# A new order for every engine, the activation table loaded first, layer-norm statistics in groups, two gates read from PSUM, and a last tile in three parts

## The chip, the cores and the metric

The kernel runs on one core of a Trainium2 chip. The core has a matrix engine (TensorE, PE in the profile; its weight loads are listed as PEld), a vector engine (VectorE, DVE), a scalar engine (ScalarE, ACT), a general engine (GpSimd, POOL), and a queue engine (SyncE, SP) that issues most DMAs. Each engine takes its own instructions in program order and waits on semaphores for the others. The metric is the device time of one execution in microseconds (us), the median of three runs.

## What is computed

```python
def _A_ref(q, k, v, shift_k, ssm_k, ssm_D):      # S = 2048 rows, D = 640 channels
    k_shift = sum(k_pad[:, t:t + S, :] * shift_k[:, ks - 1 - t] for t in range(4))
    kv = k_shift * v
    y = irfft(rfft(kv, 2 * S) * rfft(ssm_k, 2 * S))[:S]   # long convolution, per channel
    y = y + kv * ssm_D
    return q * y

x = A_q
h = x + _A_ref(layernorm(x), A_k, A_v, A_shift_k, A_ssm_k, A_ssm_D)
h2 = h + mish(layernorm(h) @ w1 + b1) @ w2               # 640 -> 1728 -> 640
```

`_A_ref` gets the normalised x as q, so the convolution's result y is multiplied ("gated") by the normalised row and added to x. Then comes an ordinary feed-forward block with the activation Mish.

## The kernel before

The long convolution is done as a two-step Fourier transform written as matrix products. The 640 channels are five blocks of 128, put in three chunks: chunk 0 is block 0, chunk 1 is blocks 1 and 2, chunk 2 is blocks 3 and 4. The 2048 rows are 16 tiles of 128. The program is a list of named operations; each name stands for a group of instructions on one engine. In the order in which data passes:

- `k1pe`, `k1ev`, `dadd` (L540, L374/L372, L549): transpose the filter, evict it from PSUM, add the direct term. `s1kpe`, `s1kev` (L466/467): first transform step of the filter; `s2kpe`, `s2kev` (L573): its second step, 22 groups of 6 frequencies. `sw` (L588/589): DMAs that make a copy of the filter's spectrum with even and odd partitions exchanged.
- `ktpe`, `ktev`, `ktsh` (L496, L505): transposed k. `wsh` (L423): the shift weights. `kspe` (L519/520): the four-tap shift as matmuls; `kv` (L525): its result times v, ten operations on DVE.
- `s1vpe`/`s1vev` and `s2vpe`/`s2vev` (L466/467, L609, evicted at L372 or L374): both transform steps of kv, 20 groups each.
- `p2` and `p1` (L629, L625): the complex product of spectrum and filter, 40 operations on bf16 data in SBUF. `p1_c_i` needs `p2_c_i`, because it overwrites what `p2_c_i` reads. They run on DVE, four of them on POOL.
- `i1pe`/`i1ev` (L660/661): first inverse step, 20 groups; those of a chunk need all its `p1` and `p2`. `gate` (L636) is a small POOL operation that waits for all products.
- per tile t: `ln1_t` (L697 to L699: two statistics, an aggregation, and the addition of epsilon on DVE), `ln1pt` (L703, L704: power -1/2 and a scaled mean on POOL), `lnxt` (the normalised tile, ACT or POOL); `i2pa/b/c` (L724: second inverse step), `yt` (eviction, L372/L374), `wbt` (times `lnx`, L735), `ht` (plus x, L739), `bnt` (L744 to L746), `powt` (POOL, L749), `hct` (L754), `trpet` (L762), `trevt` (eviction).
- the feed-forward block in units of 256, 256, 512, 512, 512 rows: `m1pe` (L797, L793), `hb` (Mish on ACT, L806), `m2pe` (L818), `res` (DVE adds the matmul's result in PSUM to x, L824), `d_out` (the DMA out). The last tile, 15, is in two halves of 320 columns: `m2a`, `resa`, `d_outa`, then `m2b`, `resb`, `d_outb`.

PSUM is used as a ring of four tiles of 1024 fp32 columns. An operation that needs one waits until an earlier holder is evicted; tiles of `i2p` may hold three at most.

The order of the work is written out by hand at the head of the file as one long list, `ORDER`, of `name:engine` (t is PE, a is ACT, v is DVE, p is POOL, d is the SP queue's DMAs). A planner walks the list, gives each operation a start time from a table of costs, assigns the PSUM tiles, and the operations are then emitted sorted by these start times. So within an engine the list decides the order; between engines the start times decide which instruction is emitted first, and dependencies (who waits for whom on a tile) are found from the emitted order:

```python
order = _schedule(ops)
order.sort(key=lambda o: (o.start, seq[id(o)]))
```

ScalarE evaluates functions from a table. The program builder puts a table load before the first copy and another before the first Mish; `warm` is a Mish of two columns that is there only to place the second load.

Of the kernel before, what the change touches and what calls it, by code (L numbers as in the profile page):

```python
# [36 lines left out]
ktsh2:p s2kev_15:a kspe4_1:t kv4_1:v s2kpe_14:t s2kev_14:a sw1_0:d kspe2_0:t s2kpe_13:t s2kev_13:a s2kpe_16:t kspe1_0:t kv2_0:v s1vpe2_0:t s2kev_16:a
s1vev2_0:a kv1_0:v s1vpe2_2:t s1vev2_2:v s1vpe2_3:t s1vev2_3:a s1vpe1_0:t s1vev1_0:v s1vpe1_3:t s1vev1_3:a s1vpe1_2:t s1vev1_2:a s1vpe1_1:t s1vpe2_1:t
s1vev2_1:a s2kpe_20:t s1vev1_1:v s2kpe_17:t s2kev_17:a s2kev_20:v kspe3_0:t s2kpe_18:t s2vpe1_2:t kspe0_1:t s2kev_18:a s2vev1_2:a sw1_1:d p2_1_2:p
s2vpe1_1:t s2vev1_1:a kv3_0:v s2vpe1_3:t s2vev1_3:a kspe4_0:t ln1_1:v s2vpe1_4:t s2vev1_4:a kv0_1:v kv4_0:v p2_1_3:v s2vpe1_6:t s2vev1_6:a kspe0_0:t  # L40
s2vpe1_0:t s2vev1_0:a p1_1_2:v p1_1_3:p kv0_0:v kspe3_1:t d_x2:d warm:a kv3_1:v sw0_1:d s2vpe1_7:t s2vev1_7:a s1vpe4_1:t s1vev4_1:a p2_1_1:v p2_1_0:v
# [8 lines left out]
i1pe2_7:t ln1_6:v d_small:p i1ev1_6:a gate:p lnx3:a i1ev2_5:a ln1p2:p ln1p1:p ln1_7:v i1ev2_7:a i1pe2_1:t i1ev2_1:a i1pe2_4:t i1ev2_4:v ln1_4:v  # L50
i1pe2_2:t i1ev2_2:a i1pe2_0:t i1ev2_0:a lnx1:p i1pe2_3:t i1ev2_3:v lnx2:p ln1p7:p ln1p6:p lnx6:p i1pe2_6:t ln1_12:v i2pa0:t i2pb0:t i2pa1:t ln1p4:p
i2pb1:t i1ev2_6:a lnx0:p i2pc1:t y1:a i2pc0:t y0:v lnx4:p b1pe:t wb1:v i2pa12:t i2pb12:t c_b1:a i2pc12:t y12:a wb0:v h0:v bn0:v i2pa3:t i2pb3:t
i2pc3:t y3:a i2pa2:t i2pb2:t i2pc2:t h1:p bn1:v i2pa6:t pow0:p hc0:v i2pb6:t y2:a i2pc6:t y6:a i2pa8:t i2pb8:t i2pc8:t y8:a i2pa11:t i2pb11:t i2pc11:t
y11:a i2pa5:t i2pb5:t i2pc5:t y5:a i2pa4:t i2pb4:t i2pc4:t y4:a i2pa13:t i2pb13:t i2pc13:t y13:a i2pa15:t i2pb15:t i2pc15:t y15:a pow1:p trpe0:t hc1:v
wb2:v i2pa7:t trev0:a i2pb7:t trpe1:t i2pc7:t trev1:v y7:a wb3:v i2pa10:t i2pb10:t i2pc10:t y10:a m1pe0_0:t m1pe0_2:t hb0_0:a m1pe0_4:t hb0_4:a
hb0_2:a h2:v bn2:v h3:p bn3:v pow2:p hc2:v m1pe0_1:t hb0_1:a pow3:p hc3:v m1pe0_6:t wb4:v h4:p trpe2:t trpe3:t lnx7:a trev2:v m1pe0_3:t hb0_6:a
ln1_10:v bn4:v ln1_5:v m1pe0_5:t wb7:p h7:p trev3:a m1pe1_1:t m1pe1_3:t wb6:v hb0_3:a h6:v hb1_1:a hb0_5:a ln1p5:p bn6:v m1pe1_4:t lnx5:a pow4:p bn7:v
hb1_3:a wb5:v h5:v bn5:v hb1_4:a m1pe1_6:t hb1_6:a pow7:p pow6:p hc4:v hc6:v hc7:v m2pe0:t trpe4:t trev4:a trpe6:t ln1_8:v trev6:a ln1p8:p ln1p10:p
ln1_11:v m1pe1_0:t ln1p11:p trpe7:t trev7:a res0:v pow5:p hb1_0:a hc5:v lnx10:a wb10:v h10:v m2pe1:t trpe5:t trev5:v m1pe1_5:t lnx11:a m1pe2_2:t
lnx8:a wb8:p h8:p wb11:v h11:v bn11:v res1:v m1pe2_0:t bn8:v pow8:p hc8:v hb2_2:a ln1_15:v ln1p15:p hb1_5:a ln1p12:p lnx12:p bn10:v pow10:p wb12:p  # L60
lnx15:p m1pe2_6:t h12:v bn12:v hb2_6:a m1pe2_5:t hb2_5:a m1pe1_2:t hb2_0:a hb1_2:a m1pe2_3:t hb2_3:a pow12:p ln1_13:v ln1p13:p i2pa9:t pow11:p i2pb9:t
# [4 lines left out]
hc13:v hc15:v trpe15:t trev15:v m1pe3_3:t hb3_3:a trpe14:t trev14:v trpe13:t trev13:a m2pe5:t res5:v d_out5:d m1pe3_4:t hb3_4:a m1pe4_5:t hb4_5:a
m1pe4_4:t hb4_4:a m1pe4_1:t hb4_1:a m1pe4_2:t hb4_2:a m1pe4_3:t hb4_3:a m2pe8:t res8:v d_out8:d m1pe4_6:t hb4_6:a m1pe4_0:t hb4_0:a m2pe10:t m2pe14:t
res14:v d_out14:d res10:v d_out10:d m2pe12:t res12:v m2pe11:t res11:v m2pe13:t res13:v d_out13:d d_out12:d m2pe9:t res9:v d_out9:d d_out11:d m2ape15:t
resa15:v d_outa15:d m2bpe15:t resb15:v d_outb15:d
# [119 lines left out]
def _dve2(n):  # L189
    return 0.06 + 0.000527 * n  # L190
# [58 lines left out]
def kernel(  # L249
# [133 lines left out]
    def emit_warm(e):
        nc.vector.memset(warm[:], 0.0)
        nc.scalar.activation(warm[:], warm[:], ACT.Mish)
# [491 lines left out]
```

## Time and profile before

| what | value |
|---|---|
| median of 3 runs | 232.85 us (232.59 to 233.19) |
| the profiled execution | 232.84 us |
| its span from first to last instruction | 231.1 us |
| PE, DVE, ACT, POOL busy | 219.0, 145.0, 137.8, 69.6 us |
| granted TensorE clock | 1.00 throughout |
| last product `p1_2_2` on DVE | 83.57 to 84.26 us |
| first feed-forward matmul `m1pe0_0` | 101.82 us |
| last feed-forward matmul ends | 227.56 us |

Times on the page are counted from the start of the span. The 1.74 us between the span and the execution's time lie around it. "Idle before" of a group is the time its engine stood still ahead of it, and the releaser is what it stood still for. The chain of waits is followed back from the last instruction, so a piece in it is work that set the end; a piece of "issue" in it is time with nothing to wait for.

### The profile page before, as it was taken

The page shows a single profiled execution, that of the slowest core. Times are in us where ns is not written, and L with a number is a line of the kernel's source. Part 1 is how long each engine was busy: PE and PEld are TensorE (multiplying, and loading weights), DVE is VectorE, ACT ScalarE, POOL GpSimd, SP SyncE. Part 2 cuts the span into 40 slices and gives each one's busy share as a digit, 9 for nine tenths or more (in the row PEclk, how much of TensorE's full clock was granted, in tenths as well). Part 3 has the DMA queues.
Part 4 walks back from the last instruction along what each step waited for, and adds up shares of the span by engine and source line. Part 5 has one row for each costly group of instructions (what it writes and reads, how often), then busy time and mean ns, then how long its engine had stood idle before and what let it go on. Part 6 is the DMA issues. An engine that isn't in the chain of part 4 may idle for free.

```text
span 231.1 us, 6508 instructions
## 1 busy us (share of the span) xinstructions
PE 219.0 (95%) x2835; PEld 167.3 (72%) x2835; DVE 145.0 (63%) x277; ACT 137.8 (60%) x187; POOL 69.6 (30%) x98
## 2 busy tenths in 40 slices
PE   7999999997889989989999999999999999999993
PEld 2898999897789979878876455777446546577772
DVE  0888999899999998987997837554641100104121
ACT  2399999999999997887745586111355254300000
POOL 0002993036620039446547186305320000000000
PEclk9999999999999999999999999999999999999999
DMA  6999997437966299200000000012000000001012
GB/s 216 380 353 375 427 413 238 129 109 244 291 175 223 54 414 373 84 1 3 0 0 3 1 0 3 24 53 96 19 11 3 28 0 0 31 0 57 3 58 85
DMA packets 19215, 28.74 MB, mean 124 GB/s; under 512 B 1137, under 2 KB 15602, under 8 KB 18802
## 3 DMA queue, kind: packets, MB, share of 16 engines
q1 hardware_dynamic: 18896, 28.17, 34.7%
q8 instruction: 22, 0.36, 0.6%
q10 hardware_dynamic: 194, 0.15, 0.2%
q14 instruction: 7, 0.06, 0.1%
q0 software_dynamic: 96, 0.00, 0.0%
HBM read 20.45 MB, written 2.62 MB: 100 GB/s over the span
## 4 chain that ended last, share of the span: by engine, by line
PE 71%; DVE 18%; ACT 5%; issue 4%; POOL 0%; DVEq 0%
PE ps L818 26%; PE ps L797 25%; ACT uv L372 4%; DVE uv L374 3%; DVE uv L625 3%; DVE uk L374 3%; PE ps L496 2%; DVE rb L629 2%; PE ps L573 2%; PE ps L540 2%; PE ps L762 2%; PE ps L394 2%; PE ps L660 2%; PE ps L661 2%; PE ps L466 2%
## 5 line engine op out<-in xcount | busy, mean ns | idle before, releaser
L818 PE MATMUL ps<-rn,uv 128*128 128x320 bf16 x448 | 62.3, 299 | 0.0
L797 PE MATMUL ps<-G 128*128 128x512 bf16 (+1 forms) x325 | 58.3, 336 | 0.0
L806 ACT ACTIVATE uv<-ps,b1s 128x512 bf16<-128x512 f32 (+1 forms) x70 | 36.7, 592 | 35.7 <-PE ps L797 28.1
L818 PEld LDWEIGHTS <-uv 128*128 128x128 bf16 x448 | 43.5, 98 | 16.9
L372 ACT CAST uk<-ps 128x1024 bf16<-128x1024 f32 (+2 forms) x47 | 43.9, 1061 | 9.0 <-PE ps L467 6.4
L797 PEld LDWEIGHTS <-G 128*128 128x128 bf16 x325 | 31.4, 98 | 23.0 <-issue 0.4
L372 ACT CAST uv<-ps 128x1024 bf16<-128x1024 f32 x32 | 30.2, 1072 | 0.3 <-PE ps L467 0.3
L824 DVE TENSOR_TENSOR xa<-ps,xa 128x640 bf16<-128x640 f32 x6 | 4.9, 823 | 26.7 <-PE ps L818 26.7
L660 PE MATMUL ps<-a,uv 128*128 128x128 bf16 x160 | 18.7, 219 | 1.2 <-DVE uv L625 1.1
L660 PEld LDWEIGHTS <-uv 128*128 128x128 bf16 x160 | 17.9, 113 | 1.3 <-DVE uv L625 1.3
L824 DVE TENSOR_TENSOR xb<-ps,xb 128x640 bf16<-128x640 f32 (+1 forms) x7 | 4.9, 727 | 21.9 <-PE ps L818 21.9
L374 DVE CAST uk<-ps 128x1024 bf16<-128x1024 f32 (+1 forms) x15 | 17.6, 1197 | 1.0 <-PE ps L661 0.6
L749 POOL TENSOR_TENSOR r<-ve,mhalf 128x1 f32<-128x1 f32 x16 | 9.3, 585 | 15.1 <-DVE ve L746 15.1
L703 POOL TENSOR_TENSOR r<-ve,mhalf 128x1 f32<-128x1 f32 x16 | 9.0, 562 | 14.4 <-DVE ve L699 14.4
L609 PE MATMUL ps<-uv,G 128*128 128x64 bf16 (+1 forms) x384 | 12.4, 186 | 1.0 <-issue 0.7
L466 PE MATMUL ps<-cst,ra 128*64 128x128 bf16 x160 | 10.7, 219 | 2.4 <-ACT uv L372 1.3
L525 DVE TENSOR_TENSOR ra<-ps,rb 128x1024 bf16<-128x1024 f32 x10 | 12.0, 1222 | 1.3 <-PE ps L520 1.3
L609 PEld LDWEIGHTS <-G 128*128 128x128 bf16 x384 | 11.6, 96 | 1.3 <-issue 1.1
L372 ACT COPY G<-ps 128x640 bf16<-128x640 bf16 x8 | 5.5, 698 | 11.6 <-PE ps L762 11.6
L372 ACT CAST rb<-ps 128x640 bf16<-128x640 f32 x15 | 9.4, 726 | 4.9 <-PE ps L724 4.9
L625 DVE TENSOR_TENSOR uv<-uv,uk 128x1024 bf16<-128x1024 bf16 x17 | 11.5, 690 | 0.8
L573 PE MATMUL ps<-uk,G 128*128 128x160 bf16 x128 | 10.8, 230 | 0.2
(111 smaller groups left out, 384.2 us busy)
## 6 DMA issues: line engine op xcount, KB each, us to landing
G<-tab_g SPq DMA_DIRECT2D x8, 512.0 KB, 8.2
rn<-in_A_ssm_k_dram SPq DMA_DIRECT2D x5, 512.0 KB, 6.7
ra<-in_A_k_dram SPq DMA_DIRECT2D x4, 640.0 KB, 9.2
rb<-in_A_v_dram SPq DMA_DIRECT2D x2, 1280.0 KB, 14.4
G<-in_B_w_dram SPq DMA_DIRECT2D x5, 432.0 KB, 4.6
rn<-in_B_w_dram SPq DMA_DIRECT2D x1, 2080.0 KB, 12.3
rn<-uk SPq DMA_DIRECT2D x4, 512.0 KB, 4.0
rb<-uk SPq DMA_DIRECT2D x4, 512.0 KB, 8.0
```

The lines of the kernel that those rows point to most:

```text
L372: nc.scalar.copy(o, i)
L374: nc.vector.tensor_copy(o, i)
L466: nc.tensor.matmul(ps[0:64, dgl, :], lhs, mc, start=True, stop=True)
L525: nc.vector.tensor_tensor(kv_w[:, m, :, 8 * h:8 * h + 8, :], rt.tile.rearrange("p (l t d) -> p d t l", l=4, t=8), raw_v[:, 8 * h:8 * h + 8 ...
L573: nc.tensor.matmul(ps[:, o:o + 160], g_v[:, f, :], KA[:, :, f, :], start=True, stop=True)
L609: nc.tensor.matmul(ps[:, fl * st:fl * st + n], g_v[:, f0 + fl, :], V[c.i][:, :, f0 + fl, :], start=True, stop=True)
L625: eng.tensor_tensor(v, v, K[c.i][:, :, f0:f1, :], ALU.mult)
L660: nc.tensor.matmul(pz[:, dgl, :], V[c.i][:, dg // 4, :, dg % 4], a12[:, 0, :], start=True, stop=False)
L797: nc.tensor.matmul(ph[:, i * 512:i * 512 + w], w1[:, dc, fc * P:fc * P + P], lnhT_of(u)[:, dc, 0:w], start=(dc == 0), stop=(dc == NDC - 1))
L806: nc.scalar.activation(hb_of(u)[:, fc, 0:n], rt.tile[:, i * 512:i * 512 + n], ACT.Mish, bias=b1s[:, fc:fc + 1], scale=1.0)
L818: nc.tensor.matmul(po[:, a * 512:a * 512 + 320], hb_of(u)[:, fc, o - x * w // 2:o - x * w // 2 + P], w2[:, fc + x, a * 320:a * 320 + 320], ...
L824: nc.vector.tensor_tensor(x, rt.tile[:].rearrange("p (a d) -> p a d", a=2)[:, n, 0:320], x, ALU.add)
```

## The change

The change has five parts.

1. `warm` is moved from the middle of ACT's list (behind 44 evictions) to its head, behind ACT's three DMA issues, and the filter's first evictions are made to depend on it. Then the program holds one table load, for Mish, ahead of the first copy, instead of two.
2. The additions of epsilon and the POOL operations of the first layer norm are made for groups of tiles (0-1, 2-3, 4-7, 8-11, 12-15) instead of one tile at a time. A group's `ln1p` is now three POOL instructions (power, product, factor -1), and a `lnx` needs the statistics of its whole group.
3. Tiles 0 and 1 have no `y`: a new `wf` on DVE multiplies `lnx` with the second inverse step's result as it stands in PSUM.
4. The last tile's second matmul, addition and output are in parts of 320, 224 and 96 columns.
5. The list `ORDER` is replaced. Every operation keeps its content, but which of DVE, ACT and POOL does an eviction or product, and when, is new throughout.

```diff
+LN1 = [(0, 2), (2, 4), (4, 8), (8, 12), (12, 16)]
+TAIL = [(0, 320), (320, 224), (544, 96)]
+FUSED = (0, 1)
...
-    OP("warm", ("act", 0.3), emit=emit_warm, prio=0)
...
+    c_warm = OP("warm", ("act", 1.7), [d_id], emit=emit_warm, prio=0)
...
-        k1 = OP(f"k1ev{b}", EVB(2048), [k1_pes[b]] + ([k1_pes[b - 3]] if b >= 3 else []), uses=[rt], emit=evf, prio=9.5)
+        k1 = OP(f"k1ev{b}", EVB(2048), [k1_pes[b], c_warm] + ([k1_pes[b - 3]] if b >= 3 else []), uses=[rt], emit=evf, prio=9.5)
...
+    for b, (t0, t1) in enumerate(LN1):
...
+        def ln1e(e, t0=t0, t1=t1):
+            (nc.gpsimd if e == "pool" else nc.vector).tensor_scalar(ve1[:, t0:t1], mv1[:, t0:t1, 1], EPS, None, ALU.add)
+        o_le = OP(f"ln1e{b}", [("dve", 0.17), ("pool", 0.3)], lss, emit=ln1e)
+
+        def ln1p(e, t0=t0, t1=t1):
+            nc.gpsimd.tensor_tensor(r1[:, t0:t1], ve1[:, t0:t1], mhalf[:, t0:t1], ALU.pow)
+            nc.gpsimd.tensor_tensor(nmr1[:, t0:t1], mv1[:, t0:t1, 0], r1[:, t0:t1], ALU.mult)
+            nc.gpsimd.tensor_scalar(nmr1[:, t0:t1], nmr1[:, t0:t1], -1.0, None, ALU.mult)
+        ln1ps.append(OP(f"ln1p{b}", ("pool", 1.5), [o_le, c_kz], emit=ln1p))
     for t2 in range(NT):
...
-            nc.vector.tensor_scalar(ve1[:, t2:t2 + 1], mv1[:, t2, 1:2], EPS, None, ALU.add)
...
-            nc.gpsimd.tensor_tensor(r1[:, t2:t2 + 1], ve1[:, t2:t2 + 1], mhalf[:, 0:1], ALU.pow)
-            nc.gpsimd.tensor_scalar(nmr1[:, t2:t2 + 1], mv1[:, t2, 0:1], r1[:, t2:t2 + 1], -1.0, ALU.mult, ALU.mult)
...
+        fused = t2 in FUSED
+        o_y = o_pe if fused else OP(f"y{t2}", EV(D), [o_pe], allocs=[tt_rt], uses=[rt, i2], emit=yf, prio=pr)
...
+            if fused:
+                tt_rt.tile = slot(tt_rt, tt_s)
+                v = lambda x: x.rearrange("p (d b l) -> p b d l", l=4, b=5)
+                nc.vector.tensor_tensor(v(tt_rt.tile), rt.tile[:, 0:D].rearrange("p (b d l) -> p b d l", b=5, l=4), v(lnx_rt.tile), ALU.mult)
+                return
...
-            for a in range(2):
-                o_pe2 = OP(f"m2{'ab'[a]}pe{t2}", ("pe", 1.905), hbs + [d_w2, w2_z, o_pe2], allocs=[] if a else [rt], uses=[rt] if a else [], emit=(lambda e, f=pe2, a=a: f(e, cols=(a,))), prio=100 + u + 0.5)
+            for i, (a, n) in enumerate(TAIL):
+                o_pe2 = OP(f"m2{'abc'[i]}pe{t2}", ("pe", 14 * _mm(n) + 0.005), hbs + [d_w2, w2_z, o_pe2], allocs=[] if i else [rt], uses=[rt] if i else [], emit=(lambda e, f=pe2, a=a, n=n: f(e, cols=((a, n),))), prio=100 + u + 0.5)
...
```

From the two lists, the stretches that the prediction speaks of, each in its engine's own order:

```text
DVE, from the fifth kv on, before:
kv1_0 s1vev2_2 s1vev1_0 s1vev1_1 s2kev_20 kv3_0 ln1_1 kv0_1 kv4_0 p2_1_3 p1_1_2 kv0_0 kv3_1 p2_1_1 p2_1_0 p1_1_1
s1vev4_0 s1vev3_0 p2_1_7 s1vev3_1 s1vev3_3 p2_1_6 p1_1_6 p2_1_4 p2_0_3 p1_1_4 p1_0_3 p2_1_5 p1_1_5 p2_0_1 p1_0_1
s2vev2_0 p2_2_0 p2_0_0 p1_0_0 p2_0_2 p1_0_2 p2_2_6 p2_2_3 p1_2_3 p2_2_5 p1_2_5 p2_2_1 p1_2_0 p1_2_1 p1_2_6 p2_2_7
p1_2_7 p2_2_4 p1_2_4 p2_2_2 p1_2_2 i1ev1_2 ln1_6 ln1_7 i1ev2_4 ln1_4 i1ev2_3 ln1_12 y0 wb1 wb0 h0 bn0 bn1 hc0 hc1 wb2
DVE, from the fifth kv on, after:
kv1_0 kv2_0 s1vev1_0 s1vev1_1 s1vev2_1 kv4_0 kv0_0 kv3_1 kv3_0 p1_1_2 s1vev0_1 s1vev0_0 p1_1_0 s1vev0_2 s1vev4_1
p2_1_6 p2_1_1 p2_1_3 s1vev3_0 s1vev3_2 p2_0_2 p1_1_1 p2_1_4 p1_1_5 p2_0_3 p1_1_7 p1_1_3 p1_1_6 p1_0_2 p1_1_4 p2_0_0
p2_2_4 p2_2_5 p2_2_6 p2_2_1 p2_0_1 p1_0_3 p1_0_1 p1_0_0 p2_2_0 p1_2_6 p2_2_7 p1_2_0 p2_2_3 p2_2_2 p1_2_5 p1_2_2
p1_2_4 p1_2_1 p1_2_3 p1_2_7 i1ev1_0 ln1_12 i1ev2_2 i1ev2_1 ln1_4 ln1_5 ln1_7 ln1_6 wf0 wf1 h0 bn0 bn1 hc0 hc1 trev0
wb3 h3 wb2 bn3 bn2 hc2 hc3 trev2 wb4 h4 wb7 bn4 ln1_10 hc4 ln1_8 ln1_13 ln1_11 h5 h6 bn6 ln1_9 res1 hc6
PE, first feed-forward matmuls, before:
m1pe0_0 m1pe0_2 m1pe0_4 m1pe0_1 m1pe0_6 trpe2 trpe3 m1pe0_3 m1pe0_5 m1pe1_1 m1pe1_3 m1pe1_4 m1pe1_6 m2pe0 trpe4
PE, first feed-forward matmuls, after:
m1pe0_2 m1pe0_4 m1pe0_3 m1pe0_0 trpe2 m1pe0_6 trpe3 m1pe0_5 m1pe0_1 m1pe1_3 m1pe1_0 m1pe1_4 trpe4 m2pe1 m1pe1_2
m1pe1_1 trpe6 m2pe0 trpe7 trpe5 m1pe1_5 m1pe1_6 m1pe2_4
POOL, around the first gates, after:
gate ln1p1 lnx3 ln1p0 lnx0 lnx1 ln1e2 ln1p2 h1 pow0 pow1 h2 pow3 pow2 h7 pow4 wb5 wb6
```

Elsewhere: of 22 `s2kev`, DVE has one instead of five; of five `k1ev` it has all instead of three; of five `ktev` all instead of four; of 20 `s1vev` nine instead of seven; of 20 `s2vev` none instead of one. ACT has the rest. In the built program the last part's first matmul `m2c` carries a wait on DVE.

More of the change, by code (lines that the diff above doesn't have):

```diff
@@ L38 @@
[L38 to L41, printed above, removed]
@@ L50 @@
[L50 to L53, printed above, removed]
@@ L54 @@
[L54 to L61, printed above, removed]
@@ L66 @@
[L66 to L69, printed above, removed]
+d_off:d d_n2:d d_id:a cz:v d_n0:d wz:v wm:t cfpe:t k1pe2:t kz:p coef:v wsh2:p warm:a k1ev2:v dadd2:v k1pe0:t s1kpe2_2:t s1kev2_2:a s1kpe2_3:t
@@ new lines @@
+m1pe0_2:t hb0_2:a m1pe0_4:t m1pe0_3:t m1pe0_0:t lnx7:a hc2:v hc3:v trpe2:t trev2:v hb0_3:a lnx4:a wb4:v h4:v hb0_0:a hb0_4:a m1pe0_6:t wb7:v h7:p
+trpe3:t hb0_6:a bn4:v pow4:p ln1_10:v trev3:a lnx6:a lnx5:a m1pe0_5:t hc4:v hb0_5:a m1pe0_1:t ln1_8:v m1pe1_3:t m1pe1_0:t wb5:p hb0_1:a m1pe1_4:t
+ln1_13:v hb1_0:a wb6:p ln1_11:v h5:v trpe4:t m2pe1:t h6:v bn6:v pow6:p ln1_9:v res1:v d_out1:d hc6:v bn7:v bn5:v hb1_3:a m1pe1_2:t trev4:a pow7:p
+pow5:p hc5:v hc7:v hb1_4:a m1pe1_1:t hb1_1:a ln1_15:v ln1_14:v ln1e4:v trpe6:t m2pe0:t trpe7:t trev7:v ln1p4:p lnx12:p lnx13:p ln1e3:v ln1p3:p lnx8:p
```

114 lines of the change are left out of this document (68 added, 46 removed).

## The prediction

> **What bounds the kernel now.** I read the page's busy shares first, then busy time by stretches, the chain of waits, and the timelines of DVE, ACT and SP.
>
> ```profile
> 60.00:70.00 10.00, 8.77 (x299) 8.27 (x294) 9.75 (x15) 10.00 (x13) 3.83 (x4) 1.00 0.72 198
> 70.00:80.00 10.00, 9.86 (x195) 9.49 (x192) 9.69 (x15) 10.00 (x13) 0.00 (x0) 1.00 0.46 144
> ...
> 115.00:130.00 15.00, 15.00 (x114) 10.10 (x113) 13.18 (x32) 8.45 (x16) 7.04 (x11) 1.00 0.00 1
> ```
>
> The columns are the stretch, its length, then busy us of PE, PEld, DVE, ACT and POOL. From 60 to 80 DVE and ACT are both full: evictions and products. From 101.82 to 227.56 PE is never idle, so the second half's length is a fixed 125.7 us of matmuls. The kernel ends earlier only if the feed-forward block starts earlier, if less of PE's work is left at that point, or if the tail shrinks.
>
> ```profile
> 83.57 0.70 DVE uv L625
> 84.32 0.25 PE ps L660
> ...
> 101.82 5.04 PE ps L797 x45
> ...
> 200.92 26.64 PE ps L818 x196
> 227.58 0.49 DVE xb L824
> 228.07 0.40 DVEq L872
> ```
>
> This is the chain of waits: start, length, what. The last product ends at 84.26, PE then starts the last inverse-step chunk (it had waited 1.1 us), and 17.56 us later the block begins. I call the end of the last product P.
>
> **The front: from kv to P.** DVE sets P. Its timeline gives the prices:
>
> ```profile
> 52.42 0.69 DVE L625 TENSOR_TENSOR uv<-uv,uk 128x1024 bf16<-128x1024 bf16 x1
> 53.02 2.36 DVE L525 TENSOR_TENSOR ra<-ps,rb 128x1024 bf16<-128x1024 f32 x2
> ...
> 60.91 2.36 DVE L374 CAST uv<-ps 128x1024 bf16<-128x1024 f32 x2
> 63.18 0.68 DVE L629 TENSOR_TENSOR rn<-rn,uv 128x1024 bf16<-128x1024 bf16 x1
> 63.90 0.69 DVE L625 TENSOR_TENSOR uv<-uv,uk 128x1024 bf16<-128x1024 bf16 x1
> 64.51 0.69 DVE L629 TENSOR_TENSOR rn<-rn,uv 128x1024 bf16<-128x1024 bf16 x1
> 65.11 0.68 DVE L629 TENSOR_TENSOR xa<-xa,uv 128x1024 bf16<-128x1024 bf16 x1
> ```
>
> An eviction or kv takes 1.18 us (2.36 for two). A product is followed 0.60 us later by an independent one (64.51 to 65.11), but a `p1` right behind its own `p2` starts 0.72 to 0.80 later (63.18 to 63.90): 0.15 extra. After `p1_1_2` (53.02) the old list has 2 kv, 5 evictions and 34 products, ten of them such pairs: 7 x 1.18 + 34 x 0.605 + 10 x 0.15 = 30.3 us; it took 31.24, so 0.95 went to waits. The new list has, after `p1_1_2`, 6 evictions and 35 products, no pair adjacent: 7.1 + 21.2 = 28.3, with the same waits 29.2. That is 2.0 less.
>
> When does the new list get there? PE fills the stretch before: from 31.3 to 40.7 the chain runs through its filter and shift matmuls without a break. At 41.2, when the fifth kv starts, the old list has done 19 of 22 filter groups and 5 shift groups; the new one does all 22 and 6 ahead of its sixth kv: 3 x 0.42 (one group, x6 in the chain) + 0.78 (one shift group, 33.82 to 34.60) = 2.0, so 43.2. Then kv 1.2, three evictions 3.5, four kv 4.7, one product 0.65: 53.25, 0.2 later than before. Net -1.8, P at 82.5.
>
> ACT must keep up, and here the **table load** counts:
>
> ```profile
> 49.34 4.70 ACT L372 CAST uv<-ps 128x1024 bf16<-128x1024 f32 x5
> 54.06 1.28 ACT L385 ACT_TABLE_LOAD   x1
> 55.35 0.20 ACT L385 ACTIVATE warm<-warm 128x2 f32<-128x2 f32 x1
> 55.47 5.57 ACT L372 CAST uv<-ps 128x1024 bf16<-128x1024 f32 x6
> ```
>
> Load and warm hold ACT from 54.06 to 55.47, 1.41 us. At the head of the list they take the place of the load before, at 2.24 to 3.52; ACT's first eviction is at 9.69, so they cost nothing there. (The Trainium skill, page ScalarE: Activation LUTs, section What ACT_TABLE_LOAD costs, gives about 1.28 us plus a drain of 1.38 for each switch. The load agrees; the drain does not show here, the next copy follows warm by 0.12. By the page 1.25 us more would be won; the row decides.) The new ACT list has, from about 44.2 on, 31 evictions of kv's transforms and 3 of the inverse step up to `s2vev2_3`: 34 x 0.93 + 0.5 for the wait on chunk 1 = 76.3, then 8 inverse evictions at 0.95 (8.56 for nine before): 83.9. `p2_2_3`, which needs 76.3, stands eight products before P, at 77.7: 1.4 of cover. The last inverse eviction is one PE group behind, so PE reaches the last chunk at about 82.7. With the load still there it would be 84.1 and DVE's gain lost. I take -1.6; the bounds are -2.2 (ACT's and PE's queues leave no more) and +0.8 (the matmuls before kv lose a us more to PSUM tiles, no pair gain).
>
> **From P to the feed-forward block.** DVE: before, three evictions and four statistics of 1.23 us; after, three and five of 1.16 (the addition of epsilon shifts its successor by only 0.07: it starts at 86.47, the next at 86.54). So `wf0` starts at P+9.3; `y0` started at P+9.2.
>
> ```profile
> 93.48 0.83 DVE L374 CAST rb<-ps 128x640 bf16<-128x640 f32 x1
> 94.22 0.88 DVE L735 TENSOR_TENSOR rb<-rb,ra 128x640 bf16<-128x640 bf16 x2
> 95.14 1.57 DVE L739 TENSOR_TENSOR x<-rb,x 128x640 bf16<-128x640 bf16 x1
> ```
>
> From `y0` to `h0` took 1.66. A product from PSUM of 640 columns is not in the trace as such; the nearest row is `res` (0.82, successor after 0.73), the dearer is kv, 1.18 x 640/1024 = 0.74. Two `wf` are 1.5: the gates win 0.1. ACT loses `y1` (0.69), which stands beside other evictions. On POOL, `ln1e2` and `ln1p2` now stand ahead of `h1`: 0.3 + power 0.56 + product and factor 0.27 each with gaps, 1.7, so `h1` runs P+11.0 to P+12.6; `bn1` wants it at P+13.7. If the power costs by column (four times 0.56), `h1` ends at 14.3 and 0.6 is lost; I take 0. The grouped rest on POOL (16 x 0.87 becomes 5 x some 1.4) is off the path. One more tile's second inverse step (0.55, eight matmuls at 137.03) is done before the block, which starts 0.3 later for it: -0.2 in all, bounds -0.5 and +0.6.
>
> **Inside the block.** The old list has 15.3 us of matmuls between `m1pe0_0` and `trpe4`, the new one 11.2 from `m1pe0_2`. DVE's queue from `hc0`, with 0.48 per `wb` and `h`, 1.24 per `bn`, 0.45 per `hc`, 1.16 per `ln1_10`, and the waits for POOL's `h2` (1.4), `pow2` (0.6) and `h7`, has `hc4` done 9.4 us after the block's start: 2 us of cover. `trpe6` has 0.3 (17.4 against 17.7), `trev7` 0.1. A stall of 0.3 is likely, 0 to 2.5 possible: +0.3.
>
> **The tail.**
>
> ```profile
> 223.78 0.82 DVE L824 TENSOR_TENSOR xa<-ps,xa 128x640 bf16<-128x640 f32 x1 [2.98 <-PE ps L818]
> ...
> 227.58 0.89 DVE L824 TENSOR_TENSOR xb<-ps,xb 128x320 bf16<-128x320 f32 x2 [2.98 <-PE ps L818]
> 228.10 0.81 SPq L836 DMA_DIRECT2D out_dram<-xb  x2
> ```
>
> This speaks against part 4. `resa` could have run at 225.7, when `m2a` was done, but both halves run at 227.58, behind `m2b`: the wait is on the whole PSUM tile. In the new list `resa` is emitted after `m2b` and before `m2c`. So it waits for `m2b`, and `m2c`, which writes the same tile, waits for it. From the start of `m2a`, with 0.1357 us per 320-column matmul (3.80 for 28): `m2b` ends at 14 x (0.1357 + 0.095) plus 0.17 of pipeline = 3.40; `resa` to 3.91; PE idle until then and 0.06 more; `m2c` 14 x 0.0425 + 0.15 = 0.75 to 4.72; `resb` and `resc` 0.30 + 0.26 to 5.30. Before, the last addition ended at 4.87. The three output issues (0.4 each) follow each other, so the last starts at 5.57, not 4.9. A DMA of 160 KB lands after 1.8, of 80 KB after 1.6; the 24 KB part by that trend 0.15 sooner. Sum +0.5, bounds +0.3 and +0.8. (The Trainium skill, DMA: Bandwidth & Descriptors, section Bandwidth, calls transfers under 64 KB descriptor-dominated: the part would land no sooner, an estimate of +0.65 by that page. No run shows a 24 KB output yet.)
>
> **Sum.** -1.6 - 0.2 + 0.3 + 0.5 = -1.0 on a span of 231.1: 230.1, with 1.74 around it 231.8 us. The profiled execution, 232.84, is the median's equal (232.85). Its own range is 231.0 to 232.6.
>
> **Rivals.** *The front gives nothing*: the filter matmuls, all moved ahead of the kv's, lose 1.6 us to PSUM tiles. For it: ACT alone evicts 21 of 22 groups at 0.87 each, 18.3 us, where DVE took five before. Against it: PE needs as long for its part. Time 232.84 + 0.6 = 233.4. *PE waits in the block (slower)*: DVE's additions and gates run at 1.57 and 1.35 instead of 0.48 when POOL adds or gates at once (95.14 above; 124.96 and 126.34 likewise). The new queue keeps them apart by a few tenths; two or three collisions make `hc4` and `hc6` 2 to 3 us late, and beyond 0.3 us at `trpe6` each us is PE's. Time 231.8 + 2.2 = 234.0. Against it: before, PE lost nothing there. *The parts do overlap*, if the wait is on columns: last addition 0.26 after the last matmul instead of 0.89, tail -0.6: 230.7. Against it: the row at 227.58.
>
> **How the numbers follow.** Forecast 0.53, front gives nothing 0.22, PE waits 0.17, parts overlap 0.08. Faster or slower counts from 0.3%, 0.7 us: 232.15 and 233.55; nearer is no difference that a measurement here shows. A seventh of the forecast's range and most of the first rival lie within: faster 0.53, same 0.26, slower 0.21. The range, 230.2 to 233.8, takes in the first rival and the overlap.
>
> **What would show it.** Right: one table load, at the start; last product near 82.6; the block's first matmul within 18 us of it; PE idle some 0.6 us before the 96-column matmuls, with the first addition inside the gap. Wrong: the last product at 84 or later; PE idle in the block above 0.5 us; the first addition before the 224-column matmuls end.

## The result, and the profile after

The changed kernel takes 234.44 us (median of 4 runs, 234.27 to 234.77) where the kernel before takes 232.77 (232.59 to 233.19): a ratio of 1.0071, 95% interval 1.0052 to 1.0090. It is slower by 1.7 us, against a forecast of 231.8 and a range that ended at 233.8. The profiled execution has 234.30 us and a span of 232.5, 1.4 more than before. Where the 1.4 went, counted from the two traces (P is the end of the last product, as in the prediction):

| stretch | before | after | difference | predicted |
|---|---|---|---|---|
| start to P | 84.27 | 86.09 | +1.82 | -1.6 |
| P to the first feed-forward matmul | 17.55 | 17.12 | -0.43 | -0.2 |
| that matmul to the 544th column of the last tile | 125.17 | 124.38 | -0.79 | +0.3 |
| from there to the end of the span | 4.08 | 4.91 | +0.83 | +0.5 |

The 544th column is where the second of the three new parts ends; for the kernel before it is worked out, 96/320 of the second half's 1.9 us ahead of its end at 227.56. The first line holds the error: it missed by 3.4 us, while the other three together came out 1.0 better than forecast. Without it the kernel would have come out 0.4 faster.

Busy time by stretches shows where (columns as in the prediction: busy us of PE, PEld, DVE, ACT and POOL).

```profile
60.00:70.00 10.00, 7.45 (x244) 7.01 (x243) 10.00 (x12) 7.33 (x8) 2.50 (x1) 1.00 0.78 279
70.00:80.00 10.00, 8.56 (x189) 7.99 (x190) 10.00 (x18) 10.00 (x12) 0.00 (x0) 1.00 0.39 134
```

DVE is busier than before (10.00 for 9.75) and finishes fewer instructions (12 for 15 in the first row), while ACT and PE, which had 10.00 and 8.77, fall to 7.33 and 7.45. So DVE's instructions have become longer. Its timeline and POOL's name them, first DVE's, then POOL's:

```profile
53.67 0.68 DVE L629 TENSOR_TENSOR uv<-uv,uk 128x1024 bf16<-128x1024 bf16 x1
54.27 2.35 DVE L377 CAST uv<-ps 128x1024 bf16<-128x1024 f32 x2
56.53 2.63 DVE L629 TENSOR_TENSOR uv<-uv,uk 128x1024 bf16<-128x1024 bf16 x1
59.08 2.34 DVE L377 CAST uv<-ps 128x1024 bf16<-128x1024 f32 x2
61.35 3.81 DVE L633 TENSOR_TENSOR rn<-rn,uv 128x1024 bf16<-128x1024 bf16 x3
```

```profile
54.14 2.20 POOL L633 TENSOR_TENSOR rn<-rn,uv 128x1024 bf16<-128x1024 bf16 x1 [0.91 <-ACT uv L375]
56.31 0.22 POOL L707 TENSOR_SCALAR ve<-mv 128x2 f32<-128x2 f32 x1
56.49 2.12 POOL L633 TENSOR_TENSOR rn<-rn,uv 128x1024 bf16<-128x1024 bf16 x1
62.11 2.50 POOL L633 TENSOR_TENSOR rn<-rn,uv 128x1024 bf16<-128x1024 bf16 x1 [3.50 <-ACT uv L375]
```

A product (lines 625 and 629 before, 629 and 633 now) takes 0.68. `p1_1_0` at 56.53 takes 2.63: POOL's product `p2_1_5` began 0.04 earlier and ended at 58.61, and `p1_1_0` ended 0.55 after that. At 61.35 three products take 3.81 instead of 1.88: the first two get done, then POOL's `p2_1_7` has its turn until 64.61, and the third ends 0.55 later, at 65.16. In the same lines the casts from PSUM at 54.27 stand beside POOL's 54.14 and take their normal 2.35 for two. So a DVE product and a POOL product on SBUF tiles exclude each other, whole instruction by whole instruction, and a DVE operation that reads PSUM isn't held up. The two meetings cost DVE 1.95 + 1.93 = 3.9 us. (The Trainium skill, SBUF — State Buffer, section SBUF: two separate sides, states just that: one port pair is shared by the two engines, the lock is exclusive, it is held for the whole instruction by whoever starts first, and it concerns DVE operations in a two-port performance mode and, against a GpSimd operation that reads SBUF, those with two SBUF inputs. The trace agrees, with 2.63 for 0.68.)

Before, POOL did four such products too. First POOL, then DVE beside the first of them, in the kernel before:

```profile
49.59 2.13 POOL L629 TENSOR_TENSOR rn<-rn,uv 128x1024 bf16<-128x1024 bf16 x1 [12.90 <-ACT uv L372]
52.58 2.51 POOL L625 TENSOR_TENSOR uv<-uv,uk 128x1024 bf16<-128x1024 bf16 x1 [0.86 <-DVE rn L629]
56.66 2.50 POOL L625 TENSOR_TENSOR uv<-uv,uk 128x1024 bf16<-128x1024 bf16 x1 [1.57 <-DVE rn L629]
61.05 2.12 POOL L625 TENSOR_TENSOR uv<-uv,uk 128x1024 bf16<-128x1024 bf16 x1 [1.89 <-ACT uv L372]
```

```profile
49.55 2.35 DVE L525 TENSOR_TENSOR ra<-ps,rb 128x1024 bf16<-128x1024 f32 x2
51.82 0.68 DVE L629 TENSOR_TENSOR rn<-rn,uv 128x1024 bf16<-128x1024 bf16 x1
```

They stood nearly wholly beside DVE's kv and casts; DVE's next product started at 51.82 and 63.18, within 0.1 of the end of the first and the last of them. The two of 2.5 started beside a DVE product that was already running, and there POOL waited. The old order was spaced around them. The new one was not.

What waited for what, from 40 to 86 us (us in total, times, longest):

```profile
ACT uv L375 <- PE ps L613: 4.2, 4, 1.6
PE ps L613 <- DVE uv L377: 3.9, 3, 1.9
DVE uv L377 <- PE ps L471: 1.4, 2, 0.8
```

The delay spreads: the casts queued behind the slow products are late (PE waits 3.9 us for them), PE's second-step groups are late, and ACT waits 4.2 us for those. With both POOL products on DVE (a_dve_products, below) the same two waits are 0.8 and 1.5 us. The last row is another, smaller loss, taken up below.

The other steps, from the timelines of single engines. First ACT's table load, at the start:

```profile
2.25 1.28 ACT L388 ACT_TABLE_LOAD   x1 [2.25 <-issue]
```

Then DVE's two `wf` and `h0`, and POOL's power on four columns and `h1` beside them:

```profile
95.43 1.56 DVE L750 TENSOR_TENSOR rb<-ps,ra 128x640 bf16<-128x640 f32 x2 [0.93 <-PE ps L735]
96.90 0.48 DVE L756 TENSOR_TENSOR x<-rb,x 128x640 bf16<-128x640 bf16 x1
```

```profile
94.91 1.03 POOL L711 TENSOR_TENSOR r<-ve,mhalf 128x4 f32<-128x4 f32 x1
...
97.07 1.57 POOL L756 TENSOR_TENSOR x<-rb,x 128x640 bf16<-128x640 bf16 x1 [0.52 <-DVE rb L750]
```

And the tail, on DVE, PE and SP's queue:

```profile
227.61 0.49 DVE L847 TENSOR_TENSOR xb<-ps,xb 128x320 bf16<-128x320 f32 x1 [2.42 <-PE ps L840]
228.95 0.56 DVE L847 TENSOR_TENSOR xb<-ps,xb 128x224 bf16<-128x224 f32 x2 [0.84 <-PE ps L840]
```

```profile
228.16 0.76 PE L840 MATMUL ps<-rn,uv 128*128 128x96 bf16 x14 [0.58 <-DVE xb L847]
```

```profile
228.13 2.04 SPq L862 DMA_DIRECT2D out_dram<-xb  x3
```

One load is left, at the start. The addition `h0` takes 0.48 where it took 1.57, because POOL's `h1` now starts 0.17 after it: `h1` waits for `wf1` (the releaser in its row), which is DVE's last operation ahead of `h0`, where before `wb1` was done first and `h1` had a lead. And `resa` waits for `m2b`, `m2c` for `resa` (0.58 of idle PE), as the prediction had it.

### The profile page after: what moved, and what is told of

Read it like the earlier page. It is cut to its first block, busy times and chain, and to the rows that moved or that the text cites. A ratio compares the mean times of both kernels' runs of the same rounds, so it can differ in the third digit from the quotient of the medians.

```text
span 232.5 us, 6500 instructions
## 1 busy us (share of the span) xinstructions
PE 217.5 (94%) x2842; PEld 168.0 (72%) x2849; DVE 142.8 (61%) x260; ACT 133.0 (57%) x186; POOL 64.6 (28%) x86
## 4 chain that ended last, share of the span: by engine, by line
PE 78%; DVE 12%; ACT 4%; issue 3%; DMA 2%; DVEq 0%; SPq 0%
PE ps L840 26%; PE ps L814 24%; PE ps L577 4%; PE ps L735 4%; DVE uv L377 3%; PE ps L665 3%; PE ps L664 3%; PE ps L470 2%; ACT uk L375 2%; PE ps L500 2%; DVE uv L629 2%; PE ps L779 2%; DMA ra<-in_A_k_dram 2%; PE ps L396 2%; PE ps L523 2%
## 5 line engine op out<-in xcount | busy, mean ns | idle before, releaser
L840 PE MATMUL ps<-rn,uv 128*128 128x320 bf16 (+2 forms) x462 | 62.4, 295 | 0.6 <-DVE xb L847 0.6
L375 ACT CAST uk<-ps 128x1024 bf16<-128x1024 f32 (+2 forms) x51 | 46.8, 1007 | 10.7 <-PE ps L471 8.8
L375 ACT CAST uv<-ps 128x1024 bf16<-128x1024 f32 x31 | 29.1, 1044 | 4.2 <-PE ps L613 4.2
L850 DVE TENSOR_TENSOR xb<-ps,xb 128x640 bf16<-128x640 f32 x5 | 4.1, 825 | 38.9 <-PE ps L840 38.9
L766 POOL TENSOR_TENSOR r<-ve,mhalf 128x1 f32<-128x1 f32 x16 | 9.0, 562 | 20.9 <-DVE ve L763 20.9
L629 DVE TENSOR_TENSOR uv<-uv,uk 128x1024 bf16<-128x1024 bf16 x20 | 14.7, 780 | 0.0
L377 DVE CAST uk<-ps 128x1024 bf16<-128x1024 f32 (+1 forms) x11 | 13.0, 1208 | 1.5 <-PE ps L471 0.8
L633 POOL TENSOR_TENSOR rn<-rn,uv 128x1024 bf16<-128x1024 bf16 x4 | 9.0, 2240 | 15.2 <-ACT uv L375 15.2
L375 ACT COPY G<-ps 128x640 bf16<-128x640 bf16 x10 | 7.1, 720 | 10.7 <-PE ps L779 10.6
L377 DVE CAST uv<-ps 128x1024 bf16<-128x1024 f32 x9 | 10.6, 1215 | 1.4 <-PE ps L471 1.4
```

The lines of the kernel that those rows point to most:

```text
L375: nc.scalar.copy(o, i)
L377: nc.vector.tensor_copy(o, i)
L629: eng.tensor_tensor(v, v, K[c.i][:, :, f0:f1, :], ALU.mult)
L840: nc.tensor.matmul(po[:, a + a // 320 * 192:a + a // 320 * 192 + n], hb_of(u)[:, fc, o - x * w // 2:o - x * w // 2 + P], w2[:, fc + x, a:a ...
```

## The experiments

Twelve kernels ran, each compared with the kernel before on the same chip. "P" is from the profiled execution of each. Between executions with the same front P differs by up to 1.0 us (85.8 to 86.8 in the changed kernel and the three that change only its tail) and the start of the work by 0.6, so P is read with that grain. The length of the stretch from the instruction behind `p1_1_2` to P does not hang on the start.

| kernel | ratio to before (95%) | median us | P |
|---|---|---|---|
| kernel before | | 232.77 | 84.3 |
| changed kernel | 1.0071 (1.0052 to 1.0090) | 234.44 | 86.1 |
| a_dve_products | 0.9962 (0.9946 to 0.9978) | 231.96 | 83.7 |
| a_late_p1 | 1.0035 (1.0008 to 1.0062) | 233.13 | 84.7 |
| b_collide | 1.0095 (1.0071 to 1.0118) | 235.05 | 86.6 |
| b_table_first | 0.9954 (0.9931 to 0.9978) | 231.54 | 83.5 |
| a_halves | 1.0053 (1.0032 to 1.0074) | 233.84 | 85.8 |
| a_own_tiles | 1.0028 (1.0012 to 1.0044) | 233.16 | 86.3 |
| a_own_halves | 1.0023 (1.0007 to 1.0038) | 233.21 | 86.8 |
| a_wsh2_late | 1.0057 (1.0033 to 1.0081) | 234.13 | 85.8 |
| c_three | 0.9910 (0.9885 to 0.9935) | 230.51 | 83.4 |
| c_kv_early | 0.9902 (0.9873 to 0.9930) | 230.24 | 83.3 |
| c_pool_one | 0.9883 (0.9854 to 0.9913) | 229.80 | 82.6 |
| b_table_tail | 0.9915 (0.9885 to 0.9945) | 230.77 | 83.8 |

Those with a are the changed kernel with an edit, those with b the kernel before with one, those with c the changed kernel with several.

### The two products moved off POOL

```diff
-... s2vev1_6:a p2_1_5:p d_a12:d ...
+... s2vev1_6:a p2_1_5:v d_a12:d ...
-... s1vev3_0:v p2_1_7:p s1vpe3_3:t ...
+... s1vev3_0:v p2_1_7:v s1vpe3_3:t ...
```

> The changed kernel with its two chunk-1 products p2_1_5 and p2_1_7 on DVE instead of POOL. Theory (DVE and POOL products on bf16 tiles hold each other up; DVE lost about 4 us to POOL's two): DVE gets 2 x 0.60 = 1.2 us more work and loses no wait, so P goes from 86.1 to 82.7 to 84.0 (ACT, which needs to about 83.9 for the inverse evictions, may bind), the product p1_1_0 takes 0.68 instead of 2.63, and the time is 231.2 to 232.6. Rival (PE's order and the PSUM tiles bound the front, DVE only waits for them): P stays or moves by the 1.2 of more work, 86 to 87.3, time 234.4 to 235.6.

The ratio falls by 0.0109, 2.5 us, and P from 86.1 to 83.7. DVE has two products more and is done earlier:

```profile
54.51 2.35 DVE L377 CAST uv<-ps 128x1024 bf16<-128x1024 f32 x2
56.78 0.68 DVE L629 TENSOR_TENSOR uv<-uv,uk 128x1024 bf16<-128x1024 bf16 x1
57.38 0.68 DVE L633 TENSOR_TENSOR rn<-rn,uv 128x1024 bf16<-128x1024 bf16 x1
57.98 2.35 DVE L377 CAST uv<-ps 128x1024 bf16<-128x1024 f32 x2
60.24 1.88 DVE L633 TENSOR_TENSOR rn<-rn,uv 128x1024 bf16<-128x1024 bf16 x3
```

`p1_1_0` takes 0.68, the three products 1.88. From the instruction behind `p1_1_2` to P it takes 29.2 us here and 31.8 in the changed kernel: 3.9 lost less 1.2 for the two products is 2.7. The collision theory holds; the rival (PE and PSUM tiles) had P at 86 or later.

### The same work, one DVE product moved by two places

```diff
-s2vpe1_4:t p1_1_0:v s2vpe1_6:t ...
+s2vpe1_4:t s2vpe1_6:t ...
-... s1vev4_1:v s2vpe0_2:t ...
+... s1vev4_1:v p1_1_0:v s2vpe0_2:t ...
```

> The changed kernel with p1_1_0 moved two DVE operations later, behind the casts s1vev0_2 and s1vev4_1, so that no DVE product stands beside POOL's p2_1_5; the work on every engine is the same. Theory (collision): the 1.95 us of the first collision goes; P 84.0 to 84.8 if the second collision (p2_1_7) stays, and 1.5 more is won if it goes too because POOL or DVE shifts; time 232.3 to 233.2. If casts from PSUM are held up by a POOL product as much as products are, nothing is won: time 234.2 to 234.6. Rival (PE and PSUM tiles): the same 234.2 to 234.6, with p1_1_0 at 0.68.

```profile
57.12 2.36 DVE L377 CAST uv<-ps 128x1024 bf16<-128x1024 f32 x2 [0.23 <-ACT uv L375]
59.39 0.68 DVE L629 TENSOR_TENSOR uv<-uv,uk 128x1024 bf16<-128x1024 bf16 x1
59.99 3.81 DVE L633 TENSOR_TENSOR rn<-rn,uv 128x1024 bf16<-128x1024 bf16 x3
```

```profile
56.76 2.12 POOL L633 TENSOR_TENSOR rn<-rn,uv 128x1024 bf16<-128x1024 bf16 x1
60.82 2.43 POOL L633 TENSOR_TENSOR rn<-rn,uv 128x1024 bf16<-128x1024 bf16 x1 [1.94 <-ACT uv L375]
```

POOL's product at 56.76 now stands beside two casts, which take 2.36 as always, and the first collision is gone. The second stays: 3.81 for three. P is 84.7, inside the 84.0 to 84.8 expected for "the second stays", and the stretch from the instruction behind `p1_1_2` to P takes 30.2 us instead of 31.8. The ratio of 1.0035 is 0.8 us below the changed kernel's, with intervals that overlap. No work was moved to another engine here, so it is the meeting that costs, not POOL's share of the work.

### The collision made in the kernel before

```diff
-... s1vev3_0:v p2_1_7:v
+... s1vev3_0:v p2_1_7:v p2_1_6:v p2_1_4:v
-s2vev0_3:a p1_1_7:p p2_1_6:v ... p1_1_6:v p2_1_4:v ...
+s2vev0_3:a p1_1_7:p ... p1_1_6:v ...
```

> The kernel before with the DVE products p2_1_6 and p2_1_4 moved forward, right behind p2_1_7, where they stand beside POOL's product p1_1_7; work the same. Theory (collision): one of them takes 2 to 2.6 instead of 0.68, P goes from 84.3 to 85.5 to 86.3, time 234.0 to 234.8. Rival (an order of DVE's products costs nothing as long as each has its inputs): time 232.6 to 233.1.

DVE, POOL, and one row of the waits from 40 to 86 us:

```profile
60.07 3.81 DVE L629 TENSOR_TENSOR rn<-rn,uv 128x1024 bf16<-128x1024 bf16 x3
```

```profile
60.89 2.43 POOL L625 TENSOR_TENSOR uv<-uv,uk 128x1024 bf16<-128x1024 bf16 x1 [1.89 <-ACT uv L372]
```

```profile
PE ps L609 <- DVE uv L374: 2.5, 1, 2.5
```

Two products moved a few places forward cost 2.2 us (1.0095), P is 2.3 later, and the same 3.81 appears. PE's wait of 2.5 for the casts queued behind is the same knock-on as in the changed kernel. The meeting itself is 1.93 of it; DVE also waits 0.73 for ACT at 69.27, right behind a stretch in which TensorE ran at half its clock (last section). The rival (the order of the products costs nothing as long as each has its inputs) is out.

### The table load alone, in the kernel before

```diff
-cz:v d_id:a wz:v wm:t ...
+cz:v d_id:a warm:a wz:v wm:t ...
-... d_x2:d warm:a kv3_1:v ...
+... d_x2:d kv3_1:v ...
```

> The kernel before with the Mish of two columns at the head of ACT's list, so that one table load is left: part 1 of the change alone. If ACT sets the front beside DVE, the 1.41 us of load and dummy come off: P 82.9 to 83.5, time 231.5 to 232.2. If DVE alone sets it, as the prediction's count of its queue says: P 84.0 to 84.3, time 232.5 to 232.9.

0.9954, 1.1 us off, P 0.8 earlier. The load of 1.41 us stood on the path although DVE looked like the engine that sets P. From the instruction behind `p1_1_2` to P it takes 30.25 us instead of 31.24, and DVE's two waits for PE in that stretch (0.45 and 0.23, at 57.63 and 59.08 before) are gone, which fits ACT and DVE feeding each other through PE. So part 1 of the change alone makes the old kernel faster, and what the rest of the change adds to it turns that gain of 1.1 into a loss of 1.7.

### The tail

```diff
-TAIL = [(0, 320), (320, 224), (544, 96)]
+TAIL = [(0, 320), (320, 320)]
```

> The changed kernel with the last tile in two halves of 320 columns, as before. The tail (from the end of the last tile's 544th column's worth of matmuls to the end of the span) was 0.83 longer after than before. Theory (the three parts cost by the wait on the whole PSUM tile and by a third issue and landing): the tail is as before, last matmul to end of span 3.5, time 233.4 to 233.9 (0.6 to 0.9 less than the changed kernel's 234.3 to 234.5). Rival (the tail's loss comes from somewhere else, such as the end of a longer span): time 234.2 to 234.6.

```diff
             for i, (a, n) in enumerate(TAIL):
+                rt = _RT(R_PS)
...
-... allocs=[] if i else [rt], uses=[rt] if i else [], ...
+... allocs=[rt], ...
```

> The changed kernel with each of the three parts of the last tile on a PSUM tile of its own. Theory (the wait is on the whole tile): PE has no gap before the 96-column matmuls, the first addition runs while PE does the second part, the last addition (0.26) ends 0.3 after the last matmul; time 232.9 to 233.5, 0.9 to 1.4 less than the changed kernel. Rival (the three issues of 0.4 and the landings set the end, the additions don't): 0 to 0.5 less, 233.9 to 234.4.

> The changed kernel with two halves of 320 columns, each on a PSUM tile of its own. Theory: the first half's addition and output run beside the second half's matmuls, one addition of 0.49 and one issue stand behind the last matmul: last matmul to end of span 3.1 instead of 3.5 with the halves on one tile, time 233.0 to 233.5. If three parts are better than two once the tiles are apart (last addition 0.26 for 0.49), this stays 0.2 above the run with three tiles; if the number of issues and landings decides, it is equal or below it.

The halves as before win 0.4 us (1.0053; expected 0.6 to 0.9, intervals overlap), and last matmul to end of span is 3.5 as before. With a PSUM tile for each part:

```profile
226.48 0.49 DVE L847 TENSOR_TENSOR xb<-ps,xb 128x320 bf16<-128x320 f32 x1 [1.08 <-PE ps L840]
227.82 0.39 DVE L847 TENSOR_TENSOR xb<-ps,xb 128x224 bf16<-128x224 f32 x1 [0.85 <-PE ps L840]
228.42 0.26 DVE L847 TENSOR_TENSOR xb<-ps,xb 128x96 bf16<-128x96 f32 x1 [0.20 <-PE ps L840]
```

Each addition follows its own matmuls, PE has no gap, and 1.0 us is won (1.0028). That the wait is on the whole tile is shown. Three parts against two on tiles of their own is a draw (1.0028 and 1.0023): the shorter last addition (0.26 for 0.49) is not seen in the time. From the last landing to the end of the span it takes 1.20 us with three parts and 0.92 with two, which gives the shorter addition back (more on this under the tail, in the next section). The median times from issue to landing were 1.6 us for 80 KB, 1.6 for 56 KB and 1.4 to 1.5 for 24 KB.

### A tiny operation behind a POOL product

```diff
-... coef:v wsh2:p warm:a ...
+... coef:v warm:a ...
-d_n4:d dadd1:p d_k0:d ...
+d_n4:d dadd1:p wsh2:p d_k0:d ...
```

> The changed kernel with POOL's first wsh2 (2.07 us) moved behind POOL's dadd1, so that DVE's first dadd2 (1 x 128, 0.82 after, 0.21 before) no longer stands beside it. Theory (collision, here of a tiny DVE operation with a POOL product): dadd2 takes 0.21, PE's first transform matmuls start 0.6 earlier, and since PE is nearly full from 30 to 50, P comes 0.3 to 0.6 earlier and the time is 233.7 to 234.1. Rival (the start is set by the filter's DMAs, the 0.6 is waited out elsewhere): dadd2 takes 0.21 and the time stays at 234.2 to 234.6.

The first line below is the changed kernel, the second, in its own fence, this one:

```profile
7.90 0.82 DVE L553 TENSOR_TENSOR x<-x,rn 1x128 bf16<-1x128 bf16 x1
```

```profile
8.47 0.21 DVE L553 TENSOR_TENSOR x<-x,rn 1x128 bf16<-1x128 bf16 x1
```

The lock is there for one partition too: `dadd2` on 1 x 128 waits out POOL's `wsh2`. Without it the operation takes 0.21. The time is 0.3 lower with overlapping intervals, so its worth in time is not shown.

### Repairs together

c_three has the two products on DVE, `wsh2` late and three parts on tiles of their own, with the edits shown above. c_kv_early builds on it, and so does c_pool_one:

```diff
-... s1vpe1_3:t s1vev1_3:a ... s1vev2_1:v kspe4_0:t kv4_0:v ...
+... kspe4_0:t s1vpe1_3:t s1vev1_3:a ... kv4_0:v s1vev2_1:v ...
```

```diff
-... p1_1_0:v ... p2_1_5:v ... s1vev4_1:v ...
+... p2_1_5:p ... s1vev4_1:v p1_1_0:v ...
```

> The changed kernel with three repairs at once: p2_1_5 and p2_1_7 on DVE, wsh2 behind dadd1, the three last parts on PSUM tiles of their own. If the three losses stand one after another on the same chain, their gains add: 2.4 for the products (as measured alone), 1.1 to 1.3 for the tail, 0.2 to 0.5 for wsh2, so 234.3 - 3.9 = 229.9 to 230.8. If the products' gain had already used up what wsh2 gives (DVE then waits for ACT), 230.7 to 231.2.

0.9910. Against the changed kernel that is 0.0161, 3.7 us, where the three alone gave 2.5 + 1.0 + 0.3 = 3.8. That fits losses that stand one after another on one chain, so that their repairs add; of the three gains the 0.3 is not shown by itself.

> The kernel with three repairs, and kspe4_0 and kv4_0 (a shift matmul group on PE, a kv on DVE) moved ahead of s1vpe1_3 and s1vev2_1. It asks about the 1.0 us by which p1_1_2 came late: DVE stood 0.56 and 0.80 for PE's transform groups, which the prediction counted with their DVE time alone. Theory (an order problem: kv4_0 can fill the second gap): p1_1_2 and P come 0.4 to 0.8 earlier, time 0.4 to 0.8 below the kernel with three repairs. Rival (PE is full there: what goes ahead makes the rest as much later): P within 0.2, time within 0.3.

```profile
45.93 1.21 DVE L529 TENSOR_TENSOR ra<-ps,rb 128x1024 bf16<-128x1024 f32 x1
47.85 1.23 DVE L377 CAST uv<-ps 128x1024 bf16<-128x1024 f32 x1 [0.71 <-PE ps L471]
50.68 1.23 DVE L529 TENSOR_TENSOR ra<-ps,rb 128x1024 bf16<-128x1024 f32 x1 [0.47 <-PE ps L524]
52.41 1.23 DVE L529 TENSOR_TENSOR ra<-ps,rb 128x1024 bf16<-128x1024 f32 x1 [0.51 <-PE ps L524]
```

The kv at 45.93 is in the gap, and the wait returns behind it: 0.71 for the cast, 0.47 and 0.51 for the shift matmuls. Time (0.9902) and P are the same within the grain. PE is full there, and what is moved ahead makes the rest late: the rival holds for this move; no other order of the stretch was tried.

> The kernel with three repairs, but p2_1_5 back on POOL and p1_1_0 behind s1vev4_1, so that POOL's product stands beside DVE's casts from PSUM only. Theory (only products on SBUF tiles meet; casts from PSUM don't): DVE has 0.60 less to do and waits 0.2 at most, P 0.3 to 0.6 earlier than in the kernel with three repairs, time 0.2 to 0.6 below it. Rival (ACT's evictions bind by then, or casts are held up too): time equal within 0.2, or above.

POOL, then DVE:

```profile
55.98 2.12 POOL L633 TENSOR_TENSOR rn<-rn,uv 128x1024 bf16<-128x1024 bf16 x1
```

```profile
56.34 2.35 DVE L377 CAST uv<-ps 128x1024 bf16<-128x1024 f32 x2 [0.23 <-ACT uv L375]
```

The lowest time, 0.9883, 2.7 us under the kernel before. POOL's product stands beside casts again (2.12 and 2.35 for two, both undisturbed) and DVE has one product less. From the instruction behind `p1_1_2` to P it takes 28.87 us, c_three 29.14, so the trace shows 0.3 where 0.3 to 0.6 was expected; 0.2 more went into a wait for ACT. The difference in time, 0.6 us, isn't shown: the intervals overlap. It beats the kernel before and the changed kernel.

> The kernel before with the table load first and its two last halves on PSUM tiles of their own; nothing of the new order. Both gains are on the path and add: 1.1 to 1.2 for the table (as measured alone) and 0.4 for the tail (one addition of 0.49 behind the last matmul instead of 0.89, one issue instead of two), time 230.9 to 231.3. If the tail's gain is lost to the second output's landing: 231.4 to 231.7.

0.9915, a time of 230.77 just under the range expected; last matmul to end of span fell from 3.5 to 3.1, the 0.4 that was counted. The old order with these two small edits has an interval that overlaps with those of all the c kernels. What the new order, the grouped statistics and the gates from PSUM are worth once the collisions are gone is therefore not settled: the ratios of b_table_tail and c_pool_one differ by 0.0032, 0.7 us. The grouping and the gates were not tried by themselves.

## Why the prediction was wrong

**The front, -1.6, was +1.82.** This is the step that failed, and in it the line that the new list has, after `p1_1_2`, 6 evictions and 35 products, "with the same waits 29.2". The number of instructions was right, but the price of 0.60 a product holds only where no POOL product stands beside it. The new list's two late POOL products stand beside DVE products, not beside casts; the prediction put nothing down for that, and the two meetings cost 3.9 us. The stretch took 31.8. With both products on DVE it took 29.2, and that this is the forecast's own number is partly luck: that run has 37 products, 1.2 us more than the count, and DVE shows none of the 0.95 of waits. The row that tells of it was in the prediction: the second rival used `h0` at 1.57 beside POOL, and looked for such meetings in the block alone. Laid over the four POOL products of the front, the same row would have shown that the old order put each of them beside kv and casts.

**The arrival at `p1_1_2`**, forecast for 53.25, was 54.27. Its step "kv 1.2, three evictions 3.5" priced the transform groups by DVE alone; in the chain of waits PE is at the eight groups from 43.5 to 47.8, when the next shift matmuls start, and DVE waited 0.56 and 0.80 for it. c_kv_early, which put a kv into the gap, gained nothing: PE is busy there for 9.75 of the 10 us from 40 to 50. Against the counted P of 82.5 the front is 3.6 late, 1.0 of it here and 2.6 in the stretch behind.

**The table load** was rightly free at the head, and the claim that with the load in its old place DVE's gain would be lost had the right sign: alone, in the old order, moving it gave 1.1 us. In the new order the old place was not tried.

**P to the block and the block** were forecast at +0.1 together and gave -1.22. (They are taken together because matmuls done ahead of the block's first are missing inside the block.) The lock worked the other way here: with `wf1` last ahead of `h0`, POOL's `h1` came a little too late to take the pair first, and `h0` fell from 1.57 to 0.48, a gain of 1.1 that the prediction did not count. With the 0.3 of PE stalls in the block, of which the waits show nothing, that is the difference to 0.1. It is read from the traces; no run put `h1` ahead of `h0` again. One addition in the block did meet POOL (1.57 at 139.47), and PE lost nothing by it. The two `wf` took 1.56, 1.5 forecast, and POOL's power on four columns 1.03, between the bounds of 0.56 and four times that.

**The tail**, +0.5 forecast, +0.83 measured, just over its upper bound. The mechanism was right in each step up to the last issue (PE idle 0.58, three issues in 2.04). The rest is where the sum was short: from the end of the last issue to the end of the span it took 2.35 us, 2.16 before, where 0.15 less was assumed. The 24 KB part did land sooner (the number at the end is the time from issue to landing in us; the first row is the kernel before):

```profile
out_dram<-xb SPq DMA_DIRECT2D x2, 80.0 KB, 1.6
```

```profile
out_dram<-xb SPq DMA_DIRECT2D x1, 24.0 KB, 1.5
```

To two digits the last landing came 1.63 us after its issue before and 1.46 after. What the prediction put at nothing stands behind it: from that landing to the end of the span it takes 1.27 us, 0.91 before. There SyncE goes through its closing waits one by one, some 0.06 us each. In the changed kernel the wait for the last output's semaphore is the first of them and six more follow it; before, all but one were done by then. (The Trainium skill, DMA: Bandwidth & Descriptors, section Bandwidth, calls transfers under 64 KB descriptor-dominated. The estimate of +0.65 that the prediction made from it came nearer to +0.83, but by luck: its reason, a landing no sooner, is not what the trace shows, with 1.46 for 1.63.)

**The rivals.** "The front gives nothing" had the right place with the wrong mechanism: the filter matmuls ahead of the kv's lost nothing to PSUM tiles, since the sixth kv started at 42.94, forecast for 43.2. "PE waits in the block" had the right mechanism, POOL and DVE excluding each other, in the wrong place. "The parts do overlap" is out: the first addition started at 227.61, behind the second part's matmuls, and PE waited for it.

## What to carry to other kernels

Before a DVE queue is priced by its rows, lay POOL's two-input operations beside it: each DVE operation with two SBUF inputs that meets one already running waits for its end, and what queues behind it on DVE is late for PE and ACT too. Put POOL's long operations beside DVE's reads of PSUM; when there is no such place, the product is cheaper on DVE (0.6 us) than on POOL (up to 2). And change one thing at a time: here a table load whose removal gained 1.1 us in the old order sat inside a change that lost 1.7.

## What was not expected of the hardware

A stall of PE can also cost TensorE its clock. In b_collide PE stood still for 2.5 us, waiting for the casts behind the slow products, and the granted clock was lower after it (the third last column):

```profile
64.00:66.00 2.00, 0.00 (x0) 0.00 (x0) 2.00 (x2) 0.82 (x1) 1.04 (x3) 0.91 1.12 284
66.00:68.00 2.00, 1.81 (x36) 1.81 (x36) 2.00 (x5) 0.69 (x1) 0.00 (x0) 0.50 0.38 96
```

At 66 to 68 PE is busy again and runs at 0.50, from 70 on at 1.00. Seven of the fourteen profiled executions have such a dip. Each lasts 3.41 us, and the time at 1.00 ahead of it is 54.6, 61.4 or 64.9 us, which is 16, 18 or 19 times 3.41: the clock seems to be set once in every 3.41 us. Cut into stretches along these steps, the changed kernel's profiled execution (first row) and a_halves, which has the same front (second row), show how close a dip can be:

```profile
62.64:66.05 3.41, 1.68 (x54) 1.50 (x49) 3.41 (x2) 3.06 (x4) 1.97 (x1) 1.00 0.87 333
```

```profile
62.61:66.02 3.41, 1.44 (x46) 1.26 (x41) 3.41 (x3) 2.81 (x4) 1.73 (x1) 0.99 0.86 349
```

PE is busy for 1.68 us of the first and 1.44 of the second, and only the second is followed by a dip. In six of the seven dips PE was busy for 0.35 to 0.44 of the stretch ahead, and every other stretch of the fourteen executions has 0.49 or more. The seventh, in c_three, is not explained: it has no collision, and 0.68 ahead of its dip. So the stalls behind a collision can bring a dip, and how they lie on the steps of 3.41 us seems to decide; that is read from the traces alone.

Over the whole execution, two of the changed kernel's four runs had a mean clock of 0.993 and 0.992 and took 234.77 and 234.57; the two with 1.000 took 234.30 and 234.27. So a dip goes with some 0.4 us in this kernel; with two runs of each kind that is an indication, not more.
